# Sums in three steps, scores in two: replanning the interleave of an attention and a feed-forward network

## The chip, the cores and the metric

The kernel runs on one core of a Trainium2 chip. The metric is the device time of one execution in microseconds (us); a smaller number is better. The core has a matrix engine (TensorE, "PE" in the profile, with its weight loads as "PEld"), three engines for elementwise work (VectorE "DVE", ScalarE "ACT", GpSimd "POOL") and SyncE ("SP"), which issues DMAs. Each engine works through its own instructions in order and waits for others by semaphores.

## The reference, cut to what matters

For each of 8 batches and 8 heads (576 rows, head size 64, 32 memory slots):

```python
a = exp(phi - max(phi, axis=seq)); a = a / (sum(a, axis=seq) + 1e-9)  # softmax over the sequence
k_m = einsum('bhsm,bhsd->bhmd', a, k)          # sums over the sequence: 32 slots a head
v_m = einsum('bhsm,bhsd->bhmd', a, v)
scores = (q @ k_m.T) / sqrt(64)
attn = softmax(scores)                         # over the 32 slots
x = (attn @ v_m) as (4608, 512)
h = x @ w_in ; g = max(0.01 * h, h) ; out = g @ w_out     # 512 -> 2048 -> 512
```

w_in and w_out come as 8-byte floats, which the kernel puts together from pairs of words; the other inputs have 4 bytes.

## The kernel before, in words

**Attention of a batch** is cut into steps `aB.X` (B is 0 to 7; "the third batch" is a2). phi, k, v and q are loaded (phi, kv0 to kv3, q0, q1). A1 to B3 make the exponentials of phi: VectorE takes maxima (A1), PE transposes and spreads them (A2, B0), ScalarE applies exp (B20). C10 are the sums k_m and v_m: 72 f32 products, each on a 64x32 tile of PE, eight tiles side by side, over nine slices j of the rows (`slots_of`, line 654; the trace counts 144 matmuls, two for each f32 product). C2 to D6 scale and transpose the results; D2 (line 346) spreads a maximum over the partitions, from a diagonal that VectorE makes in C4. Q0 and Q1 are VectorE's transpositions of q for the two groups of heads (line 772). E1 makes the scores for both groups: 48 f32 products on 32x32 tiles, twelve side by side, 96 matmuls in the trace (`scores`, line 793); its three PSUM buffers are the whole pool `ps_a`. E20 to E22 transpose the scores out of PSUM, S01 to S08 are the softmax.

**The feed-forward network** does not multiply by v_m first: steps `Wbj.p` fold v_m of batch b into the quarter j of w_in (line 909, also on 64x32 tiles), h and l split the result in two f16 halves. Then each group of 256 rows, quarter by quarter (k counts group and quarter), goes through `pk.i` (PE, up: six or twelve matmuls, line 1104), `vk.i` (ScalarE, leaky ReLU), `sk` (VectorE, four sums), `ck`, `lk` (f16 halves by ScalarE and VectorE), and `dk.n` (PE, down: seven steps of six matmuls of 256 columns, line 1172). `xG` and `zG` combine, scale and store a group. The first three groups of rows use an older form, `P`, `V`, `C`, `L`, `O`, `Z` (lines 993 and 1061).

**The order** of all steps is written out by hand in two strings, OPENING (up to about 105 us) and LATER. The program runs them word by word under a manual schedule, so the order of the words is the order of the instructions on each engine. Between engines only semaphores hold. `FB = 2` is the number of first batches that keep f32 folds.

Of the kernel before, what the change touches and what calls it, by code (L numbers as in the profile page):

```python
# [68 lines left out]
a2.phi a2.kv2 W01.h1 W01.h0 i0.k1 a2.kv3 W01.l0 i0.k0 W01.l1 i0.k2 o0.s0 Z0.0 a2.kv0 a2.A1 Z0.1  # L69
W11.p o0.m0 Z0.2 P8.0 o0.s1 W11.h0 o0.n0 a2.A2 V8.0 P8.1 W11.l0 W11.h1 P9.0 W11.l1 V8.1 a2.kv1  # L70
C8 P9.1 V9.0 L8 V9.1 o0.s2 W02.h1 O8.0 C9 W02.h0 W02.l1 o0.m1 W02.l0 o0.m2 O8.1 L9 o0.n1 W12.p
o0.n2 o0.s3 P10.0 W12.h1 o1.s0 P10.1 W12.l1 V10.0 o3.s3 P11.0 V10.1 a2.A3 W12.h0 O9.0 V11.0
W12.l0 o1.k0 C10 o1.k1 i0.l2 a2.B0 L10 P11.1 o1.k2 o1.l1 O9.1 V11.1 W03.h1 o1.l2 W03.h0 W03.l1
P12.0 o0.m3 W03.l0 o1.l0 W13.p V12.0 C11 O10.0 W13.h0 W13.h1 W13.l0 o1.m0 W13.l1 P12.1 L11
O10.1 V12.1 o0.n3 o1.n0 o1.s1 P13.0 C12 o1.m1 o1.s2 P13.1 V13.0 o1.n1 P14.0 L12 V13.1 O11.0
o1.s3 V14.0 C13 o1.m2 a2.B10 o2.k0 P14.1 o2.k1 o2.l0 O11.1 V14.1 o2.l1 o2.k2 o1.m3 o1.n2 a2.B20
P15.0 o2.l2 L13 O12.0 o1.n3 V15.0 o2.s0 C14 a2.C10 o2.m0 o2.s1 o2.n0 o2.m1 L14 P15.1 a2.q0
o2.n1 O12.1 o2.s2 V15.1 a2.B3 o2.m2 a2.q1 P16.0 o2.s3 a2.C2 V16.0 O13.0 C15 o3.k0 o2.n2 a3.phi
o3.k1 L15 P16.1 o3.k2 o3.l0 O13.1 V16.1 o3.l2 o2.m3 o3.l1 o3.s0 P17.0 C16 O14.0 o3.s1 V17.0 L16
o3.s2 P17.1 a2.C30 o3.m1 O14.1 a2.Q0 V17.1 o3.m3 o3.m2 o3.n3 P18.0 a2.C3k o3.n2 a2.D10 V18.0  # L80
o3.n1 o3.m0 O15.0 C17 a2.D3 a2.Q1 P18.1 L17 O15.1 V18.1 a2.C31 i0.l1 C18 a2.E1 Z1.0 a2.C4 Z1.1
L18 Z1.2 P19.0 i0.l0 O16.0 a2.E21 V19.0 a2.E20 i1.k1 a3.kv2 a2.E22 o2.n3 i1.k0 a2.D2 a2.S01
a2.D11 i1.k2 P19.1 a3.kv1 a2.D4 O16.1 V19.1 a2.S02 a2.D5 a3.kv0 P20.0 C19 a2.D6 L19 O17.0 V20.0
a3.kv3 a2.S03 i1.l0 i1.l1 W20.p a2.S04 P20.1 W20.h0 O17.1 V20.1 W20.h1 W20.l0 C20 P21.0 a2.S05
O18.0 V21.0 L20 W20.l1 a2.S06 P21.1 O18.1 V21.1 i1.l2 a2.S07 o3.n0 C21 W21.p i2.k1 a3.A1 a2.S08
P22.0 i2.k0 O19.0 V22.0 L21 i2.k2 W21.h0 W21.h1 a3.A2 P22.1 i2.l0 i2.l1 O19.1 V22.1 i2.l2 C22
i3.k1 P23.0 W21.l0 i3.l1 O20.0 V23.0 i3.k0 W21.l1 L22 i3.k2 W22.p i3.l0 P23.1 W22.h0 i3.l2
O20.1 W22.l0 V23.1 a3.A3 W22.h1 C23 W23.p W22.l1 L23 p0.0 W23.h0 a3.B0 os2 v0.0 W23.l0 O21.0
W23.h1 a3.B10 W23.l1 p0.1 O21.1 v0.1 a3.B20 a3.B3 a3.C10 p0.2 a3.q0 a3.C2 v0.2 O22.0 a3.C30
a3.C3k a3.C31 a3.q1 a3.C4 a3.D11 a3.D10 a3.D2 a3.D3 p0.3 a3.D4 a4.phi O22.1 v0.3 a3.Q0 a3.D5  # L90
c0.0 p1.0 s0 p1.1 v1.0 O23.0 v1.1 l0.0 c0.1 a3.Q1 p1.2 O23.1 v1.2 l0.1 a3.D6 a4.A1 p1.3 a3.E1
v1.3 Z2.2 Z2.0 s1 Z2.1 p2.0 p2.1 a3.E22 v2.0 d0.0 a3.E21 v2.1 a3.E20 c1.0 d0.1 a4.kv0 os3 W30.p
c1.1 l1.0 p2.2 W30.h0 l1.1 d0.2 a4.kv1 v2.2 W30.h1 d0.3 a3.S01 d0.4 p2.3 a4.kv3 W30.l1 d0.5
a3.S02 v2.3 d0.6 c2.0 p3.0 s2 a4.kv2 p3.1 v3.0 d1.0 v3.1 l2.0 c2.1 d1.1 W30.l0 p3.2 l2.1 W31.p
v3.2 a3.S03 d1.2 d1.3 W31.h0 a3.S04 d1.4 W31.h1 p3.3 d1.5 v3.3 W31.l0 d1.6 c3.0 s3 p4.0 p4.1
v4.0 l3.0 a4.A2 v4.1 d2.0 c3.1 a3.S05 d2.1 p4.2 l3.1 d2.2 v4.2 d2.3 a3.S06 d2.4 p4.3 W31.l1
d2.5 a4.A3 v4.3 a3.S07 d2.6 s4 a4.B0 p5.0 a3.S08 p5.1 a4.B10 v5.0 d3.0 v5.1 d3.1 x3.p c4.0 p5.2
d3.2 v5.2 c4.1 d3.3 x3.0 d3.4 a4.B20 x3.1 p5.3 l4.0 d3.5 v5.3 x3.2 a4.C10 c5.0 l4.1 l5.0 s5
d3.6 a4.q0 p6.0 p6.1 x3.3 v6.0 d4.0 a4.B3 v6.1 c5.1 d4.1 a4.q1 p6.2 d4.2 l5.1 v6.2 z3.1 a4.C2
d4.3 a5.phi a4.C30 z3.0 d4.4 a4.Q0 p6.3 a4.C3k d4.5 v6.3 a4.D10 c6.0 s6 d4.6 a4.D3 p7.0 l6.0  # L100
p7.1 v7.0 a4.Q1 d5.0 v7.1 c6.1 d5.1 p7.2 a4.C31 l6.1 d5.2 v7.2 a4.E1 a4.C4 a5.A1 d5.3 a5.kv0
d5.4 p7.3 a4.E20 a4.E22 d5.5 v7.3 a5.kv2 a4.E21 a4.D2 c7.0 s7 a4.D11 d5.6 p8.0 a5.kv1 l7.0 p8.1
v8.0 a4.S01 d6.0 v8.1 c7.1 d6.1 a5.kv3 p8.2 l7.1 d6.2 v8.2 d6.3 a4.S02 d6.4 p8.3 a4.D4 d6.5
v8.3 a4.D5 os4 W32.p s8 d6.6 W32.h0 p9.0 W32.h1 W32.l0 p9.1 v9.0 W32.l1 d7.0 v9.1 a4.D6 d7.1
x4.p c8.0 p9.2 d7.2 v9.2 c8.1 d7.3 x4.0 d7.4 a4.S03 x4.1 p9.3 l8.0 d7.5 v9.3 x4.2 W33.p c9.0
l8.1 d7.6 W33.h1 p10.0 W33.h0 W33.l1 p10.1 W33.l0 v10.0 d8.0 x4.3 v10.1 d8.1 s9 z4.0 p10.2 d8.2
v10.2 l9.0 c9.1 d8.3 d8.4 z4.1 l9.1 p10.3 d8.5 v10.3 W40.p c10.0 s10 d8.6 W40.h1 p11.0 W40.h0
l10.0 p11.1 v11.0 a4.S04 d9.0 v11.1 c10.1 d9.1 p11.2 l10.1 d9.2 v11.2 d9.3 a4.S05 d9.4 p11.3
W40.l0 d9.5 W40.l1 v11.3 W41.p a4.S06 c11.0 a5.A2 W41.h0 d9.6 s11 a4.S07 p12.0 p12.1 v12.0
l11.0 a4.S08 d10.0 v12.1 c11.1 d10.1 W41.l0 p12.2 W41.h1 l11.1 d10.2 v12.2 d10.3 d10.4 p12.3  # L110
# [12 lines left out]
v19.0 a5.S02 d17.0 v19.1 c18.1 d17.1 W50.l0 p19.2 W50.h1 l18.1 d17.2 v19.2 a5.S03 d17.3 W50.l1
d17.4 a5.S04 p19.3 d17.5 v19.3 W51.p c19.0 s19 d17.6 W51.h0 p20.0 W51.h1 l19.0 p20.1 v20.0
d18.0 a5.S05 v20.1 c19.1 d18.1 p20.2 l19.1 d18.2 v20.2 d18.3 a5.S06 d18.4 p20.3 W51.l1 d18.5
W51.l0 v20.3 d18.6 c20.0 s20 p21.0 p21.1 v21.0 l20.0 d19.0 v21.1 d19.1 x7.p c20.1 p21.2 d19.2
v21.2 a5.S07 d19.3 x7.0 d19.4 x7.1 p21.3 a5.S08 x7.2 d19.5 l20.1 v21.3 d19.6 c21.0 p22.0 p22.1
v22.0 d20.0 v22.1 d20.1 x7.3 p22.2 s21 d20.2 v22.2 d20.3 l21.0 c21.1 d20.4 p22.3 l21.1 d20.5
v22.3 z7.1 d20.6 s22 c22.0 p23.0 p23.1 v23.0 d21.0 l22.0 v23.1 c22.1 d21.1 p23.2 l22.1 d21.2
v23.2 z7.0 d21.3 d21.4 p23.3 d21.5 v23.3 d21.6 c23.0 s23 p24.0 p24.1 v24.0 l23.0 d22.0 v24.1  # L130
c23.1 a6.A2 d22.1 a6.A3 p24.2 l23.1 a6.B0 v24.2 d22.2 a6.B10 d22.3 d22.4 a6.B20 p24.3 d22.5
v24.3 a6.B3 W52.p c24.0 d22.6 W52.h1 p25.0 W52.h0 W52.l1 p25.1 W52.l0 v25.0 d23.0 s24 v25.1
a6.C10 x8.p l24.0 c24.1 l24.1 d23.1 a6.q0 a6.C2 p25.2 a6.C30 d23.2 v25.2 a6.C3k d23.3 x8.0
a6.q1 d23.4 x8.1 a6.D10 x8.2 a6.C31 p25.3 a6.D3 a6.Q0 a7.phi d23.5 v25.3 W53.p c25.0 s25 d23.6
W53.h1 p26.0 W53.h0 p26.1 W53.l1 v26.0 d24.0 W53.l0 v26.1 c25.1 d24.1 x8.3 l25.0 p26.2 d24.2
l25.1 v26.2 z8.1 d24.3 z8.0 d24.4 a6.Q1 p26.3 d24.5 v26.3 a6.E1 c26.0 s26 l26.0 c26.1 d24.6
a7.kv3 a6.E22 p27.0 l26.1 p27.1 v27.0 d25.0 a7.kv1 v27.1 a6.E21 d25.1 a6.E20 a6.C4 p27.2 a6.D11
a6.S01 v27.2 a7.kv2 a6.D2 d25.2 d25.3 a6.D4 d25.4 a7.kv0 a6.S02 a6.D5 p27.3 d25.5 a6.D6 v27.3
d25.6 c27.0 s27 W60.p p28.0 l27.0 p28.1 v28.0 a7.A1 d26.0 v28.1 c27.1 d26.1 p28.2 W60.h1 l27.1
d26.2 v28.2 a6.S03 d26.3 W60.l1 d26.4 os6 W60.h0 p28.3 a6.S04 d26.5 v28.3 d26.6 c28.0 s28 p29.0  # L140
# [1217 lines left out]
```

## Time and profile before

| | |
|---|---|
| median of 3 runs | 663.27 us (662.59 to 666.29) |
| the profiled execution's own time | 662.05 us |
| its span, first to last instruction | 659.8 us |
| PE busy | 642.2 us (97%) |
| PE weight loads busy | 481.8 us (73%) |
| VectorE busy | 519.2 us (79%) |
| ScalarE busy | 396.3 us (60%) |
| GpSimd busy | 31.1 us (5%) |
| granted TensorE clock, mean | 0.997 |

The profile shows one execution. Busy times are shares of the span; a matmul's end is modelled, so neighbouring matmuls overlap in it, and the pace is read from starts: the time from one step's first start to the next step's first start.

### The profile page before, as it was taken

To read this page: it belongs to the slowest core of one execution; us is meant where nothing else is said; L and a number is where in the kernel's file an instruction comes from. 1 tells how busy PE (TensorE), PEld (TensorE's weight loads), DVE (VectorE), ACT (ScalarE), POOL (GpSimd) and SP (SyncE) were. 2 spreads that over 40 slices of the span, in tenths; PEclk is the share of its full clock that TensorE was granted. 3 is DMA by queue.
4 is the path that set the end of the run, shared out by engine and by line. 5 is a ranking of instruction groups with operands and counts; after the bars stand their busy time and mean duration, and the time that the engine had idled before them with its cause. 6 is when DMAs were issued, how large, how long until landed. Compare 5 with 4: busy or idle time off the path is not lost.

```text
span 659.8 us, 17603 instructions
## 1 busy us (share of the span) xinstructions
PE 642.2 (97%) x7592; PEld 481.8 (73%) x7592; DVE 519.2 (79%) x857; ACT 396.3 (60%) x677; POOL 31.1 (5%) x43
## 2 busy tenths in 40 slices
...
GB/s 292 400 314 309 232 86 121 1 51 60 192 1 82 65 157 69 178 42 33 51 93 139 40 1 33 109 177 3 34 74 33 2 33 6 30 18 16 33 2 48
DMA packets 32605, 60.38 MB, mean 92 GB/s; under 512 B 4368, under 2 KB 14608, under 8 KB 32528
## 3 DMA queue, kind: packets, MB, share of 16 engines
q1 hardware_dynamic: 32432, 59.13, 29.6%
q8 instruction: 59, 0.97, 0.6%
q10 hardware_dynamic: 96, 0.13, 0.1%
...
## 4 chain that ended last, share of the span: by engine, by line
PE 91%; DVE 5%; ACT 1%; issue 1%; DMA 1%; SPq 0%; POOL 0%; DVEq 0%; ACTq 0%; POOLq 0%
PE po L1172 31%; PE ph L1104 21%; PE po L1061 14%; PE ph L993 8%; PE ph L1172 5%; PE pa L909 4%; PE pa L654 2%; PE pa L793 2%; PE po L1206 1%; PE pa L1260 1%; DMA arena<-in_moe_w_out_dram 1%; PE pa L605 0%; DVE tm L827 0%; PE pa L346 0%; DVE t L807 0%
## 5 line engine op out<-in xcount | busy, mean ns | idle before, releaser
L1172 PEld LDWEIGHTS <-arena 128*128 128x128 f16 x2184 | 210.4, 98 | 30.4 <-issue 7.4
L1120 ACT ACTIVATE wi<-ph,g_sc 128x256 f32<-128x256 f32 (+1 forms) x224 | 98.8, 465 | 171.1 <-PE ph L1104 168.4
L1104 PE MATMUL ph<-a,w_mem 128*128 128x256 f16 (+3 forms) x1440 | 144.7, 246 | 0.0
L1104 PEld LDWEIGHTS <-w_mem 128*128 128x128 f16 x1440 | 114.4, 98 | 14.4 <-issue 3.5
L1172 PE MATMUL po<-wo,arena 128*128 128x256 f16 x936 | 122.0, 273 | 0.0
L1172 PE MATMUL po<-arena 128*128 128x256 f16 x936 | 115.5, 273 | 0.0
L1061 PE MATMUL po<-wo,arena 128*128 128x512 f16 (+1 forms) x384 | 110.9, 434 | 0.0
L1149 DVE TENSOR_TENSOR arena<-arena 128x1024 f16<-128x1024 f32 x52 | 64.1, 1233 | 25.1 <-ACT arena L1145 25.0
L1149 DVE TENSOR_TENSOR arena<-wi,arena 128x768 f16<-128x768 f32 (+1 forms) x60 | 54.3, 905 | 10.7 <-ACT arena L1145 10.7
L1141 DVE TENSOR_TENSOR arena<-wi 128x256 f32<-128x256 f32 x104 | 39.9, 425 | 24.7 <-ACT wi L1120 24.6
L1145 ACT CAST arena<-arena 128x1024 f16<-128x1024 f32 x52 | 54.4, 1046 | 2.3 <-DVE arena L1141 2.3
L993 PE MATMUL ph<-a,w_mem 128*128 128x192 f16 (+2 forms) x304 | 53.7, 323 | 1.6 <-DVE a L852 1.6
L1061 PEld LDWEIGHTS <-arena 128*128 128x128 f16 x288 | 27.8, 98 | 29.9 <-DVE wo L419 0.8
L1145 ACT CAST arena<-wi 128x768 f16<-128x768 f32 (+1 forms) x60 | 46.5, 776 | 1.7
L1141 DVE TENSOR_TENSOR arena<-wi,arena 128x256 f32<-128x256 f32 x104 | 45.8, 440 | 1.8
L876 POOL TENSOR_TENSOR a<-t,a 128x384 f16<-128x384 f32 x22 | 22.7, 1053 | 444.6 <-ACT a L871 440.4
L1172 PE MATMUL ph<-wo,arena 128*128 128x256 f16 x312 | 42.6, 273 | 0.0
L1000 ACT ACTIVATE arena<-ph,g_sc 128x384 f32<-128x384 f32 x32 | 18.6, 582 | 26.3 <-PE ph L993 21.6
L1061 PEld LDWEIGHTS po<-wo,arena 128*128 128x128 f32 x96 | 17.6, 190 | 21.0 <-issue 19.1
L909 PE MATMUL pa<-wi,vT 64*32 64x512 f16 (+1 forms) x704 | 28.9, 420 | 0.5 <-ACT vT L742 0.5
L932 ACT ACTIVATE w_mem<-pa 128x512 f16<-128x512 f32 x40 | 22.8, 596 | 8.0 <-PE pa L909 7.1
L993 PEld LDWEIGHTS <-w_mem 128*128 128x128 f16 x240 | 20.6, 98 | 9.4 <-issue 3.6
...
## 6 DMA issues: line engine op xcount, KB each, us to landing
...
```

The lines of the kernel that those rows point to most:

```text
L876: nc.gpsimd.tensor_tensor(lo[:, tb], t2[:, tb], hi[:, tb], ALU.subtract)
L909: nc.tensor.matmul(pf[g][cols, :], lhs, rhs, start=(n == 0), stop=(n == len(passes) - 1), tile_position=(g * D, hh * M),)
L932: nc.scalar.activation(halves(w16(b, j), g)[:, 0], src["w"][g] if b else w32[j][g], AF.Copy, scale=ws)
L993: nc.tensor.matmul(ph[:, t0:t0 + n * SB], lhs, rhs, start=(m == 0), stop=(m == len(seq) - 1))
L1000: nc.scalar.activation(dst, ph, AF.Prelu, scale=sc, alpha=SLOPE)
L1061: nc.tensor.matmul(po, lhs, rhs, start=(f == 0 and m == 0), stop=(f == NQ * NF - 1 and m == len(seq) - 1),)
L1104: nc.tensor.matmul(ph[:, t0:t0 + n], lhs, rhs, start=(m == 0), stop=(m == len(seq) - 1))
L1120: nc.scalar.activation(dst, ph, AF.Prelu, scale=g_sc2[:, j:j + 1], alpha=SLOPE)
L1141: nc.vector.tensor_tensor(gt[:, x], y, z, op)
L1145: nc.scalar.copy(dst[:, 0], src)
L1149: nc.vector.tensor_tensor(dst[:, 1], src, dst[:, 0], ALU.subtract)
L1172: nc.tensor.matmul(acc, g[:, x, s, u], rhs, start=(h == 0 and j == 0 and u == 0 and m == 0), stop=(j == NQ - 1 and u == 1 and m == 2), ski ...
```

## The change

The code changes in two places, both for batches 2 to 7 only. C10 becomes C10, C11 and C12, each with three of the nine slices j. E1 becomes E1 with the first group of heads and E1b with the second. The products themselves, their number and their order within the step stay; results are accumulated in the same PSUM buffers.

```diff
-        def slots_of(kinds):
+        def slots_of(kinds, js=range(KJ)):
...
-            for j in range(KJ):
+            for j in js:
...
-            steps[f"{name}C10"] = lambda: slots_of((0, 1))
+            parts = 3 if b >= FB else 1
+            for x in range(parts):
+                js = range(x * KJ // parts, (x + 1) * KJ // parts)
+                steps[f"{name}C1{x}"] = lambda js=js: slots_of((0, 1), js)
...
-        steps[f"{name}E1"] = lambda: scores((1,) if b == 0 else range(NG))
+        steps[f"{name}E1"] = lambda: scores((1,) if b == 0 else range(NG) if b < FB else (0,))
+        if b >= FB:
+            steps[f"{name}E1b"] = lambda: scores((1,))
```

LATER is a new order of the same words with the new ones between; OPENING stays. The stretch of the sixth batch, before and after:

```diff
-x5.p c12.1 p13.2 d11.2 v13.2 a5.B20 d11.3 x5.0 d11.4 x5.1 a5.C10 x5.2 l12.1 a5.B3 p13.3 a5.q0
-d11.5 v13.3 d11.6 c13.0 a5.C2 x5.3 p14.0 a5.q1 s13 p14.1 v14.0 d12.0 v14.1 d12.1 l13.0 c13.1
-p14.2 a6.phi d12.2 l13.1 v14.2 z5.0 d12.3 z5.1 a5.C30 d12.4 p14.3 a5.Q0 d12.5 v14.3 d12.6 c14.0
-s14 p15.0 p15.1 v15.0 d13.0 l14.0 v15.1 c14.1 d13.1 a5.C31 p15.2 l14.1 a5.D11 v15.2 d13.2
-a5.C3k a5.Q1 d13.3 a5.D10 d13.4 a5.C4 a5.D3 p15.3 a6.A1 a5.D2 v15.3 d13.5 c15.0 d13.6 p16.0 s15
...
-l16.0 v17.1 a5.E1 x6.p c16.1 l16.1 d15.1 a6.kv3 p17.2 a5.E22 a5.E21 d15.2 v17.2 d15.3 x6.0
+a5.B20 d12.6 s14 p15.0 a5.C10 v15.0 a5.B3 c14.0 p15.1 a5.C11 v15.1 c14.1 d13.0 l14.0 a5.C12
+l14.1 d13.1 a5.q0 a5.C2 d13.2 a5.C30 p15.2 d13.3 a5.C31 v15.2 a5.q1 a5.C4 a5.C3k d13.4 p15.3
+a5.D10 v15.3 a6.phi c15.0 s15 d13.5 a5.D3 d13.6 p16.0 l15.0 p16.1 v16.0 a5.Q0 d14.0 v16.1 c15.1
+d14.1 d14.2 l15.1 a5.E1 a5.Q1 p16.2 d14.3 v16.2 d14.4 a6.A1 a5.E1b p16.3 a6.kv3 a5.E20 d14.5
```

The last words of the order, from p54.0 on, follow each other on PE as before.

## Rows read from the trace of the kernel before

**Rows 1.** The chain of waits that ended last, share of the span by engine.
```profile
PE 91%; DVE 5%; ACT 1%; issue 1%; DMA 1%; SPq 0%; POOL 0%; DVEq 0%; ACTq 0%; POOLq 0%
```
**Rows 2.** Busy time by stretch: start:end, length, each engine's busy us (instructions), clock, DMA.
```profile
105.00:350.00 245.00, 241.58 (x2930) 174.13 (x2930) 221.22 (x349) 142.47 (x244) 9.67 (x12) 1.00 0.29 80
350.00:655.00 305.00, 304.56 (x3751) 261.68 (x3749) 222.20 (x369) 176.28 (x317) 8.96 (x11) 1.00 0.16 44
```
**Rows 3.** PE's waits from 105 us on: line, releaser, us in total, times, longest.
```profile
PE pa L654 <- issue: 2.5, 2, 1.5
PE ph L1104 <- ACT wi L1120: 0.4, 1, 0.4
PE pa L346 <- DVE mdiag L341: 0.4, 1, 0.4
```
**Rows 4.** PE in time order, ordinary steps: start, us to modelled end, operation, count.
```profile
273.47 1.48 PE L1172 MATMUL po<-arena 128*128 128x256 f16 x12
274.79 0.82 PE L1104 MATMUL ph<-a,w_mem 128*128 128x256 f16 x6
```
**Rows 5.** The same view around the seventh batch's sums, then its transpositions D10.
```profile
417.24 0.82 PE L1172 MATMUL ph<-wo,arena 128*128 128x256 f16 x6
417.99 2.25 PE L654 MATMUL pa<-arena 64*32 64x128 f32 x144
420.17 0.50 PE L1172 MATMUL po<-wo,arena 128*128 128x256 f16 x3
...
423.58 0.60 PE L719 MATMUL pa<-ident,x_k 128*96 128x128 f32 x4
424.01 0.58 PE L1104 MATMUL ph<-a,w_mem 128*128 128x192 f16 x5
```
**Rows 6.** The same view around a fold.
```profile
414.46 0.84 PE L909 MATMUL pa<-wi,vT 64*32 64x512 f16 x24
415.24 0.39 PE L1172 MATMUL po<-arena 128*128 128x256 f16 x2
```
**Rows 7.** The same view: scores, batch 0's first half; the sixth batch's whole.
```profile
15.02 1.15 PE L793 MATMUL pa<-wi,kT 32*32 32x192 f32 x48 [0.67 <-ACT kT L736]
...
354.05 1.93 PE L793 MATMUL pa<-arena,kT 32*32 32x192 f32 x96
355.91 0.28 PE L1172 MATMUL po<-wo,arena 128*128 128x256 f16 x1
```
**Rows 8.** The same view, fourth and fifth batch's sums; idle time in brackets.
```profile
205.64 2.16 PE L654 MATMUL pa<-arena 64*32 64x128 f32 x133
209.34 0.44 PE L654 MATMUL pa<-arena 64*32 64x128 f32 x11 [1.55 <-issue]
209.71 0.83 PE L1104 MATMUL ph<-a,w_mem 128*128 128x256 f16 x6
...
255.68 2.20 PE L654 MATMUL pa<-arena 64*32 64x128 f32 x139
258.82 0.41 PE L654 MATMUL pa<-arena 64*32 64x128 f32 x5 [0.94 <-issue]
259.17 0.50 PE L1172 MATMUL po<-wo,arena 128*128 128x256 f16 x3
```
**Rows 9.** Engine totals; instruction packets (span, 206 to 209.5); a stretch as rows 2.
```profile
PE 642.2 (97%) x7592; PEld 481.8 (73%) x7592; DVE 519.2 (79%) x857; ACT 396.3 (60%) x677; POOL 31.1 (5%) x43
...
q8 instruction: 59, 0.97, 0.6%
...
q8 instruction: 1, 0.02, 2.1%
...
209.34:258.81 49.48, 48.21 (x637) 37.09 (x637) 44.12 (x73) 28.00 (x50) 3.21 (x4) 1.00 0.34 100
```
**Rows 10.** VectorE in time order around the sixth batch's second transposition of q.
```profile
339.61 1.77 DVE L772 STREAM_TRANSPOSE arena<-arena 96x1536 f32<-96x1536 f32 x1
...
341.84 0.29 DVE L341 TENSOR_SCALAR mdiag<-ident,m 128x128 f32<-128x128 f32 x1
```

More of the change, by code (lines that the diff above doesn't have):

```diff
@@ L68 @@
 LATER = """
[L69 to L110, printed above, removed]
@@ L123 @@
[L123 to L140, printed above, removed]
@@ L183 @@
-d54.0 c55.1 l55.1 d54.1 d54.2 d54.3 d55.0 d55.1 d55.2 d55.3 end
+a2.phi a2.kv2 W01.h1 W01.h0 i0.k0 a2.kv1 i0.k1 W01.l1 W01.l0 i0.k2 o0.s0 Z0.0 a2.kv0 a2.A1
+o0.m0 Z0.1 W11.p Z0.2 P8.0 o0.s1 W11.h0 o0.n0 P8.1 V8.0 W11.l0 P9.0 o0.s2 a2.kv3 V8.1 W11.h1 C8
+P9.1 V9.0 L8 o0.m1 a2.A2 V9.1 W11.l1 O8.0 W02.h0 C9 W02.h1 W02.l0 o0.m2 W02.l1 O8.1 L9 o0.n1
+W12.p o0.n2 o0.s3 P10.0 W12.h0 o1.s0 a2.A3 P10.1 V10.0 W12.l0 P11.0 V10.1 o3.s3 W12.h1 O9.0 C10
+V11.0 W12.l1 o1.k1 L10 o1.k0 P11.1 o1.l1 o1.k2 O9.1 o0.m3 o1.l0 V11.1 o1.l2 W03.h0 C11 W03.h1
@@ new lines @@
+a2.B0 W03.l0 P12.0 o1.m0 W03.l1 O10.0 V12.0 L11 o0.n3 o1.n0 W13.p o1.s1 P12.1 a2.B10 W13.h0
+O10.1 V12.1 W13.l0 W13.h1 o1.m1 W13.l1 P13.0 a2.B20 o1.n1 o1.s2 P13.1 V13.0 C12 a2.C10 o1.s3
+V13.1 o1.m2 L12 P14.0 o2.k0 C13 a2.C11 V14.0 o1.n2 O11.0 o2.k1 o2.l0 o2.k2 o2.l1 o1.m3 a2.C12
+o2.l2 P14.1 L13 a2.q0 o1.n3 O11.1 V14.1 o2.s0 C14 o2.m0 a2.q1 o2.s1 P15.0 o2.n0 O12.0 L14 V15.0
+o2.m1 o2.s2 o2.n1 o2.m2 P15.1 a2.B3 O12.1 V15.1 o2.s3 a3.phi a2.C2 C15 o3.k1 P16.0 o2.n2 o3.k2
+O13.0 o3.l1 V16.0 o3.k0 o3.l2 L15 o2.m3 P16.1 o3.l0 O13.1 V16.1 o3.s0 C16 o3.s1 P17.0 L16 O14.0
@@ new lines @@
+V17.0 o3.s2 a2.C30 o3.m2 o3.m3 a2.Q0 P17.1 o3.m1 O14.1 a2.C3k o3.n3 V17.1 o3.n2 o3.m0 o3.n1
+a2.D10 C17 P18.0 a2.D3 a2.Q1 O15.0 V18.0 L17 a2.C31 P18.1 i0.l1 a2.E1 V18.1 a2.C4 O15.1 C18
+i0.l2 L18 a2.E1b Z1.2 i0.l0 Z1.1 P19.0 a2.E20 Z1.0 a2.E21 a2.D2 V19.0 a2.E22 O16.0 a2.D4 i1.k0
+i1.k1 a2.S01 a3.kv0 a2.D11 i1.k2 P19.1 i1.l1 a2.D5 O16.1 a3.kv2 V19.1 a2.S02 C19 a2.S03 P20.0
+a3.kv3 a2.D6 L19 W20.p V20.0 a2.S04 O17.0 W20.h1 a3.kv1 W20.h0 W20.l1 P20.1 a2.S05 O17.1 V20.1
+W20.l0 a2.S06 P21.0 C20 i1.l2 O18.0 V21.0 L20 a2.S07 i1.l0 P21.1 a2.S08 o3.n0 i2.k1 W21.p V21.1
@@ new lines @@
+O18.1 i2.k0 i2.k2 W21.h0 P22.0 C21 W21.h1 i2.l0 O19.0 V22.0 L21 i2.l2 P22.1 i2.l1 O19.1 W21.l0
+V22.1 i3.k1 W21.l1 C22 i3.k0 W22.p i3.l1 i3.k2 P23.0 i3.l0 W22.h0 O20.0 i3.l2 V23.0 L22 W22.h1
+W22.l1 P23.1 W22.l0 o2.n3 O20.1 V23.1 a3.A1 W23.p C23 p0.0 W23.h0 os2 a3.A2 L23 v0.0 O21.0
+W23.h1 W23.l0 W23.l1 a3.A3 p0.1 O21.1 v0.1 a3.B0 p0.2 a3.B10 O22.0 v0.2 a3.B20 p0.3 a3.B3
+a3.C10 v0.3 O22.1 c0.0 s0 a3.C11 l0.0 c0.1 p1.0 a3.C12 v1.0 l0.1 p1.1 a3.q0 a3.C2 v1.1 O23.0
+a3.C30 a3.C3k a3.C31 a3.q1 a3.C4 a3.D11 a3.D10 a3.D2 a3.D3 p1.2 a3.D4 a4.phi O23.1 v1.2 a3.Q0
@@ new lines @@
+a3.D5 p1.3 a3.D6 a3.Q1 p2.0 v1.3 a3.E1 v2.0 Z2.2 s1 p2.1 Z2.0 a3.E1b Z2.1 v2.1 a4.A1 d0.0 c1.0
+d0.1 c1.1 d0.2 a4.kv3 l1.0 p2.2 d0.3 l1.1 v2.2 d0.4 a4.kv0 a3.E21 p2.3 a3.E22 d0.5 a3.E20 v2.3
+os3 d0.6 c2.0 a4.kv2 s2 W30.p p3.0 W30.h0 l2.0 p3.1 a4.kv1 v3.0 a3.S01 d1.0 v3.1 c2.1 d1.1
+W30.l0 d1.2 W30.h1 l2.1 p3.2 W31.p v3.2 a3.S02 d1.3 W31.h1 d1.4 W31.h0 W30.l1 a3.S03 p3.3
+W31.l1 d1.5 W31.l0 v3.3 d1.6 c3.0 s3 p4.0 p4.1 v4.0 l3.0 d2.0 v4.1 c3.1 d2.1 a3.S04 d2.2 p4.2
+d2.3 l3.1 v4.2 d2.4 a3.S05 p4.3 d2.5 v4.3 d2.6 a3.S06 c4.0 p5.0 s4 p5.1 v5.0 d3.0 v5.1 a3.S07
```

131 lines of the change are left out of this document (83 added, 48 removed).

## The prediction, made before the result was known

> **What bounds the kernel now.** I first read the busy time by stretch. The written-out later order, which is all that the change touches, fills 105 to 655 us. In it PE is busy for 241.58 of the first 245 us and for 304.56 of the other 305 [rows 2]; the differences are 3.42 and 0.44, so PE is idle for 3.86 us in 550. The chain of waits says the same: 91% of the span is PE's own work [rows 1]. VectorE is the next, at 221.22 of 245 us in the first stretch and 222.20 of 305 in the second [rows 2]. Then I read PE's waits in the later order: 2.5 us of the 3.86 are called "issue" and stand at line 654, the sums, twice; 0.4 waits for ScalarE near the end, 0.4 for VectorE ahead of D2 [rows 3], the rest is shorter. So only two things can move the time: what PE's own steps cost, and the waits, above all the two at line 654.
>
> **Does "busy" mean full pace?** A row of matmuls that starts at 273.47 holds 12 products of 256 columns and the next step starts at 274.79: 1.32/12 = 0.11 us each [rows 4]. That pace holds across ordinary steps, so PE's time is the sum of its steps, and a step that grows by x delays the end by x.
>
> **What a tiled step costs at its ends.** The sums work on eight 64x32 tiles at once, the scores on twelve of 32x32; all neighbours use the whole array. Ahead of the seventh batch's sums, six products start at 417.24 and should have been fed by 417.24 + 6 x 0.11 = 417.90, yet the sums start at 417.99: 0.1 us is lost on entering. The sums last from 417.99 to 420.17, 2.18 us [rows 5]. Their content: 144 matmuls in eight tiles are 18 in depth, of 128 columns f32. Four whole-array f32 matmuls of 128 columns take from 423.58 to 424.01, 0.108 each [rows 5], so 18 take 1.95. The remaining 0.23 is the end: the tiles run out one after another before the whole array may start.
>
> **Part 1, sums in three.** No matmul is added. Each third has 48 matmuls, 6 in depth: 6 x 0.108 + 0.23 = 0.88, three make 2.64 against 2.18: +0.46 a batch. Lower bound of the end: the folds (24 matmuls, 3 in depth, of 512 columns or 3 x 0.22 = 0.66) last from 414.46 to 415.24 = 0.78 [rows 6], an end of 0.12; with that a third would last 0.77 and three 2.31, +0.13. Nothing hides these, for PE has no slack. I take 0.44, nearer to the step itself. Six batches: +2.6 (0.8 to 2.8).
>
> **Part 2, scores in two.** The score step lasts 354.05 to 355.91 = 1.86 us [rows 7]. Half of its content is at least 0.93. Batch 0 already has its scores in halves: 48 matmuls from 15.02, for 1.15 us to the modelled end of the last [rows 7]; the whole step's row says 1.93 where 1.86 passed to the next start, so 1.08 at most. Two halves cost 0 to 0.30 more; I take 0.2, nearer to the half that exists. Six batches: +1.2 (0 to 1.8).
>
> **Part 3, the entries.** In the new order every part has a whole-array step on either side (a5: C10 p15.1 C11 d13.0 C12; E1 p16.2 d14.3 d14.4 E1b), so 2 + 1 = 3 entries are added in each of six batches: 18 x 0.1 = +1.8. Lower end 0, if the new neighbours were hidden in the fill; upper 2.0.
>
> **Part 4, the two "issue" waits.** The sums of the fourth batch run from 205.64 to 209.71 = 4.07, those of the fifth from 255.68 to 259.17 = 3.49, against 2.18: 1.89 + 1.31 = 3.2 us lost. In each, PE stops with nothing to wait for, 133 and 139 matmuls in, and goes on at 209.34 and 258.82 [rows 8]. What is special there is the rate. Every matmul has its weight load, so the sums use 288 instructions in 2.18 us, where ordinary steps use 2 in 0.11, 40 in the same time. Instructions come by a queue of their own: 59 packets of 0.97 MB in all, 16 KB each, for 2 x 7592 instructions of PE [rows 9], or 257 a packet. From the end of the first stop to the end of the second there are 637 matmuls and 637 weight loads [rows 9]; with a few semaphore instructions that is 5 x 256. So both stops lie on the edge of a packet, and a packet is under way in the first (206 to 209.5 us [rows 9]). I read them as PE using up a packet inside the sums faster than the next comes. The instructions came 3.7 us after the first sums' start, and 3.1 after the second's. In the new order the same 256 instructions are 96 + some 14 + 96 + some 14 + the rest of the last third: 0.98 + 0.65 + 0.98 + 0.65 + 0.3 = 3.6 us at the fastest, and longer where the step between is one of 1.9 us. So both stops should go and none come: -3.2 (bounds 0 and -3.2).
> The Trainium skill ("Runtime: NRT & Kernel Launch", Instruction fetch mechanics) also has blocks of 16 KiB and 256 instructions, but calls the cost of crossing one mostly hidden; by that the 3.2 us would belong to something else and could stay. The trace shows 2.5 us of idle PE exactly there, so for the sum I follow the rows; the page's reading speaks for the third rival below.
>
> **Part 5, the replanned order.** The work on the other engines is the same, every step once. Without the two stops, 3.86 - 2.5 = 1.4 us of waits remain in the later order. The one ahead of D2 of the sixth batch goes: VectorE had put its 1.77 us transposition of q (339.61) before the diagonal that D2 needs (341.84) [rows 10]; in the new order that transposition, Q1, comes behind E1, which needs only Q0. The wait of 0.4 at the end stays, for the last steps are unchanged. New is that Q0 and Q1 stand three or four PE steps (2 us) ahead of E1 and E1b, where they stood half a group of rows ahead. PSUM is as full as before, but the scores hold all three shared buffers for some 2 us longer. Bounds -1.4 and +2; I take -0.4. DMA issues are the same ones in other places, and the queue of SP is mostly free in this stretch; I count nothing for them.
>
> **Sum:** 2.6 + 1.2 + 1.8 - 3.2 - 0.4 = +2.0 us on the profiled execution's 662.05: 664.05. That execution is the lowest of the four known (662.59, 663.27 and 666.29 are the others; the two in the middle average 662.9), and what is forecast is a median, so I add 0.5, about half of what lies between: **664.5 us**, 0.2% above the median of before. Less than 0.5%, 3.3 us, can't be told from no change here: same is 660.0 to 666.6. The likeliest case's own range is 662.5 to 666.5.
>
> **Rivals.**
> 1. *The ends cost little, the waits all go.* If thirds and halves cost nothing beyond their content (both lower bounds near 0) and only the entries are paid: 1.8 - 3.2 - 1.4 = -2.8, 659.8 with the 0.5; less if entries hide too. For it: no row shows so short a group of f32 tiles among whole-array steps, and the folds' end is half as long as the sums'. Against: the folds have an end all the same, and no slack covers it. 7%.
> 2. *Slower: q's transpositions become late.* Place: E1 and E1b, in each of six batches, behind Q0 and Q1 (1.77 us on VectorE [rows 10]) with some 2 us of PE work between. If what stands before them on VectorE is late by its usual wait for ScalarE, each half waits up to 1.77 and on average perhaps half: 6 x 0.9 = 5.3 more, 669.8. It decides from 0.4 us a batch on, where 664.5 becomes 666.9. For: VectorE is 90% busy in the first stretch [rows 2]. Against: after 350 us it is 73% busy, and three of the six batches lie there. 10%.
> 3. *The stops stay or move.* If they come from something other than the dense run of instructions, the change does not reach them: 664.5 + 3.2 = 667.7. For: four other sums of the same shape have none, so density alone doesn't make one. Against: the 5 x 256 between the two. 7%.
> The forecast has the remaining 76%.
>
> **Chances.** Faster by over 0.5% takes rival 1 at its better end and little else: 7%. Slower takes rivals 2 and 3, 17%, and nearly nothing of the forecast: 17%. Same: 76%. The range of 8 in 10 takes in rival 3 and the bounds -2.8 to +5 of the parts but not rival 2's full price: 661.0 to 667.7.
>
> **What would show it.** In the changed trace: PE pieces of 48 matmuls at line 654 with about 0.88 us to the next step's start, and 0.1 us before each; halves of about 1.03 us at the scores' line; no "issue" wait at line 654, and PE idle for under 2 us between 105 and 655 us, while the span is some 2 us longer, all of it as PE busy time. The forecast is wrong if thirds take under 0.78, if PE waits for VectorE or ScalarE at E1 or E1b, or if an "issue" wait of over 0.5 us remains.

## The result, and the profile after

The changed kernel takes 667.1 us (median of 16 runs, 665.56 to 669.28); the kernel before, in as many runs on the same chip, 663.61 us. The ratio is 1.005 with a 95% interval of 1.0039 to 1.0061: half a per cent slower, 2.6 to 4.0 us. The profiled execution's span went from 659.8 to 664.7 us.

That span difference of 4.9 us is not all the change's. I split it where the later order begins: at the first matmul of its first fold, 105.15 us before and 107.14 us after. The opening's words are the same in both kernels, and over eight kernels that share its instructions the later order began anywhere from 105.15 to 108.55 us. So the 2.0 us at the opening are within what the same opening varies by, one execution of each kernel. The later order, from that matmul to the last one's start, took 549.95 us before and **552.82 us** after: **+2.87 us**. This length is what I compare from here on; it is free of the opening's spread, and TensorE's granted clock in it is 1.00 in both.

Chain of waits after, by engine [as rows 1]:

```profile
PE 89%; DVE 4%; DMA 2%; ACT 2%; issue 1%; SPq 0%; POOL 0%; DVEq 0%; ACTq 0%; POOLq 0%
```

Busy time by stretch after, columns as in [rows 2]:

```profile
105.00:350.00 245.00, 243.95 (x2944) 171.58 (x2943) 217.53 (x343) 143.05 (x245) 10.10 (x12) 1.00 0.29 80
350.00:659.90 309.90, 308.98 (x3742) 263.25 (x3741) 227.49 (x378) 177.21 (x319) 8.78 (x11) 1.00 0.16 43
```

PE is idle for 1.05 + 0.92 us where it was idle for 3.86, and yet the end is later: PE waits less, but its steps have grown by more. Its waits after, from 105 us on [as rows 3]:

```profile
PE ph L1110 <- ACT wi L1126: 0.9, 2, 0.5
PE po L1178 <- DVE obs L1193: 0.4, 1, 0.4
PE pa L731 <- DVE x_v L704: 0.3, 1, 0.3
PE pa L797 <- DVE arena L776: 0.3, 1, 0.3
```

The two "issue" stops at the sums are gone. What took their place stands in the time order of PE. The fifth batch's sums [as rows 5, 8], in three parts with an ordinary step between (start, us to the modelled end, count):

```profile
266.30 0.94 PE L655 MATMUL pa<-arena 64*32 64x128 f32 x48
267.17 0.83 PE L1110 MATMUL ph<-a,w_mem 128*128 128x256 f16 x6
267.93 0.94 PE L655 MATMUL pa<-arena 64*32 64x128 f32 x48
268.80 0.83 PE L1178 MATMUL ph<-wo,arena 128*128 128x256 f16 x6
269.56 0.94 PE L655 MATMUL pa<-arena 64*32 64x128 f32 x48
270.43 0.39 PE L1178 MATMUL po<-wo,arena 128*128 128x256 f16 x2
```

Each third lasts 0.87 us from its start to the next step's (266.30 to 267.17), 2.61 together against 2.18 whole. The six matmuls between last 0.76 (267.17 to 267.93) where six at the free pace last 0.65: the entry of 0.1. The same batch's scores in halves [as rows 7]:

```profile
276.65 0.41 PE L1110 MATMUL ph<-a,obs 128*128 128x192 f16 x3
277.34 1.14 PE L797 MATMUL pa<-arena,kT 32*32 32x192 f32 x48 [0.28 <-DVE arena L776]
278.41 0.35 PE L1110 MATMUL ph<-a,w_mem 128*128 128x64 f16 x6
...
281.82 1.15 PE L797 MATMUL pa<-arena,kT 32*32 32x192 f32 x48
282.90 0.50 PE L1178 MATMUL po<-arena 128*128 128x256 f16 x3
```

A half lasts 1.07 to 1.08 us, so two are 2.16 against 1.86. The 0.28 in brackets is the one place where PE waits for a transposition of q.

### The profile page after: what moved, and what is told of

Read it like the earlier page. It is cut to its first block, busy times and chain, and to the rows that moved or that the text cites. A ratio compares the mean times of both kernels' runs of the same rounds, so it can differ in the third digit from the quotient of the medians.

```text
span 664.7 us, 17625 instructions
## 1 busy us (share of the span) xinstructions
PE 648.0 (97%) x7592; PEld 480.6 (72%) x7592; DVE 518.7 (78%) x857; ACT 395.8 (60%) x677; POOL 31.3 (5%) x43
## 4 chain that ended last, share of the span: by engine, by line
PE 89%; DVE 4%; DMA 2%; ACT 2%; issue 1%; SPq 0%; POOL 0%; DVEq 0%; ACTq 0%; POOLq 0%
PE po L1178 31%; PE ph L1110 21%; PE po L1067 12%; PE ph L999 7%; PE ph L1178 5%; PE pa L915 3%; PE pa L655 3%; PE pa L797 2%; DMA arena<-in_moe_w_out_dram 2%; PE po L1212 1%; PE pa L1266 1%; DMA arena<-in_q_dram 1%; ACT arena L396 1%; PE pa L606 0%; ACT arena L385 0%
## 5 line engine op out<-in xcount | busy, mean ns | idle before, releaser
L1178 PEld LDWEIGHTS <-arena 128*128 128x128 f16 x2184 | 209.5, 98 | 32.4 <-issue 9.5
L1178 PE MATMUL po<-arena 128*128 128x256 f16 x936 | 122.3, 273 | 0.0
L1155 DVE TENSOR_TENSOR arena<-wi,arena 128x768 f16<-128x768 f32 (+1 forms) x60 | 52.9, 881 | 10.4 <-ACT arena L1151 10.4
L776 DVE STREAM_TRANSPOSE arena<-arena 96x1536 f32<-96x1536 f32 x14 | 24.6, 1765 | 3.3 <-DMA arena<-in_q_dram 1.8
```

Of the source, the lines that this page charges most:

```text
L776: nc.vector.transpose(flat, ld["q", g].rearrange("p hh j d -> p (hh j d)"))
L1155: nc.vector.tensor_tensor(dst[:, 1], src, dst[:, 0], ALU.subtract)
L1178: nc.tensor.matmul(acc, g[:, x, s, u], rhs, start=(h == 0 and j == 0 and u == 0 and m == 0), stop=(j == NQ - 1 and u == 1 and m == 2), ski ...
```

## The experiments

All lengths are of the later order, start of its first matmul to start of its last, in one profiled execution; medians and ratios are of all executions, the ratios against the kernel before on the same chip. An "edge" is the place in PE's stream of instructions where one packet of 256 ends and the next begins.

| kernel | begins at | length | median | ratio, 95% interval |
|---|---|---|---|---|
| before | 105.15 | 549.95 | 663.61 | 1 |
| changed | 107.14 | 552.82 | 667.1 | 1.005 (1.0039 to 1.0061) |
| e1 parts adjacent | 106.85 | 550.00 | 663.89 | 0.9992 (0.9978 to 1.0007) |
| e2 sums whole | 107.70 | 550.61 | 664.66 | 1.0008 (0.9995 to 1.002) |
| e3 scores whole | 106.33 | 552.30 | 666.6 | 1.0044 (1.003 to 1.0057) |
| e4 both whole | 108.55 | 549.85 | 664.22 | 1.0007 (0.9995 to 1.0018) |
| e5 edges moved by 96 | 113.21 | 547.49 | 667.78 | 1.0056 (1.0034 to 1.0078) |
| e6 edges moved by 140 | 118.84 | 550.18 | 674.69 | 1.0158 (1.0134 to 1.0183) |
| e7 sums whole, early | 106.85 | 550.48 | 664.13 | 1.0005 (0.9992 to 1.0018) |
| e8 cuts in the old order | 106.22 | 555.50 | 669.66 | 1.0095 (1.0072 to 1.0119) |
| e9 edges moved by 208 | 112.10 | 547.34 | 665.11 | 1.0016 (1.0 to 1.0031) |
| e10 edges moved late, by 96 | 108.65 | 547.69 | 661.15 | 0.9948 (0.993 to 0.9967) |
| e11 changed, edges at sums | 106.42 | 553.56 | 667.12 | 1.0047 (1.003 to 1.0064) |

**e1: is it the cut or what stands between?** The changed code with the old order, parts adjacent.

```diff
-x5.p c12.1 p13.2 d11.2 v13.2 a5.B20 d11.3 x5.0 d11.4 x5.1 a5.C10 x5.2 l12.1 a5.B3 p13.3 a5.q0
+x5.p c12.1 p13.2 d11.2 v13.2 a5.B20 d11.3 x5.0 d11.4 x5.1 a5.C10 a5.C11 a5.C12 x5.2 l12.1 ...
```

> The old order, with the three parts of the sums and the two of the scores directly behind one another. Measure: the later order's length, from the first matmul of its first fold to the last matmul of the kernel (before: 105.15 to 655.10 = 549.95 us; changed: 107.14 to 659.96 = 552.82). Theory (a part costs only where whole-array work stands on both sides): as before, 549.5 to 550.5, ratio to before 0.999 to 1.001, and the two issue stops stand in the same two batches' sums (fourth and fifth), since the instructions and their places are the same. Rival 1 (cutting a step costs by itself, more semaphores and instructions): 553 or more, at least 3 us longer. Rival 2 (the stops are chance and not tied to the place of an instruction in the stream): none, or in other batches.

Measured: 550.00 us, ratio 0.9992. A cut between parts that stay neighbours is free. And both stops are back, after the same number of matmuls as in [rows 8]:

```profile
207.53 2.16 PE L651 MATMUL pa<-arena 64*32 64x128 f32 x133
211.06 0.44 PE L651 MATMUL pa<-arena 64*32 64x128 f32 x11 [1.37 <-issue]
...
257.40 2.20 PE L651 MATMUL pa<-arena 64*32 64x128 f32 x139
260.54 0.41 PE L651 MATMUL pa<-arena 64*32 64x128 f32 x5 [0.94 <-issue]
```

They are no chance: 133 and 139 matmuls in, in another execution of another build.

**e2 to e4: undo the cuts one at a time in the new order.** All parts stand where the last one stood.

```diff
-a5.B20 d12.6 s14 p15.0 a5.C10 v15.0 a5.B3 c14.0 p15.1 a5.C11 v15.1 c14.1 d13.0 l14.0 a5.C12
+a5.B20 d12.6 s14 p15.0 v15.0 a5.B3 c14.0 p15.1 v15.1 c14.1 d13.0 l14.0 a5.C10 a5.C11 a5.C12
...
-d14.1 d14.2 l15.1 a5.E1 a5.Q1 p16.2 d14.3 v16.2 d14.4 a6.A1 a5.E1b
+d14.1 d14.2 l15.1 a5.Q1 p16.2 d14.3 v16.2 d14.4 a6.A1 a5.E1 a5.E1b
```

> The new order, but all three parts of the sums stand together where the last stood; the scores stay in halves. Theory: the drains at the ends of thirds (18 x 0.87 against 6 x 2.18 = 2.6) and 12 entries (12 x 0.105 = 1.3) go: 552.8 - 3.9 = 548.9 us for the later order, ratio to before 0.998 to 1.000. The instruction packets' edges fall about 100 or more instructions behind the start of each batch's sums, so that less than a packet is used up inside; no issue stop. Rival (the stops come with whole sums, wherever the edges fall): two stops or so, 1.3 to 1.9 us each, 551.5 to 552.5.

> The new order, but both halves of the scores stand where the second stood; the sums stay in thirds. Theory: 12 halves of 1.08 against 6 x 1.86 (1.8) and 6 entries (0.6) go: 552.8 - 2.4 = 550.4 us. Rival (the halves hide a late transposition of q, the second group's, which now holds up the whole step): PE waits for VectorE ahead of the scores in the fourth, fifth and sixth batch, together up to 2.3 us, and 552.7 remains.

> The new order with sums and scores whole, each where its last part stood. Theory: the savings of the two one-sided kernels add up: 552.8 - 3.9 - 2.4 = 546.5 us, 3.4 below before, of which 3.2 are the two stops that this order does not have; ratio to before 0.994. With the waits for q's second transposition up to 548.8, ratio 0.998. Rival (the new order's interleave needs the parts: longer tiled steps starve ScalarE and VectorE and PE waits for them elsewhere): 550 or more without any issue stop.

Measured: 550.61, 552.30 and 549.85. The savings came short by 1.7, 1.9 and 3.4 us, and not by stops (none is in the later order of these traces), and hardly by q (0.5 us in one place in e2, where the changed kernel has 0.3; nothing in e3 and e4). PE's busy time in the later order did fall, from 550.9 to 547.2, 549.1 and 545.4 us; its idle time rose from 2.0 to 3.4, 3.2 and 4.4, which is most of what is missing. e4 is nearest to its rival, which had named such waits. e2 around the sixth batch:

```profile
334.21 0.82 PE L1106 MATMUL ph<-a,w_mem 128*128 128x256 f16 x6
335.65 0.82 PE L1106 MATMUL ph<-a,w_mem 128*128 128x256 f16 x6 [0.62 <-ACT wi L1122]
```

This is p15.0 and then p15.1. In the new order v15.0 (ScalarE) comes between the two, and PE's second step does not start before v15.0 has ended (335.13 + 0.47 = 335.60). In the changed kernel C10 stands in that gap. e3 has the same with the scores, 2.4 us in four waits:

```profile
PE ph L1106 <- ACT wi L1122: 2.4, 4, 0.9
```

So the new order spends the parts as cover for waits which it makes itself; the old order has p15.0 p15.1 v15.0 and no such wait. My rival for e3 had the size (552.7) but named the wrong partner (q instead of v).

**e7: whole sums, at the first part's place.**

```diff
+a5.B20 d12.6 s14 p15.0 a5.C10 a5.C11 a5.C12 v15.0 a5.B3 c14.0 p15.1 v15.1 c14.1 d13.0 l14.0
```

> The changed kernel with all three parts of the sums where the first stood; the scores stay in halves. In the kernel with the sums at the last part's place PE waited 0.79 us twice between two up steps of one group, where a part of the sums had stood between them. Theory: those waits are gone, the packets' edges fall at instruction 126 or later of each sums, so no stop: 552.82 - 2.7 (ends) - 1.3 (12 entries) = 548.8 us, ratio to before 0.997 to 0.999. Rival (the waits in the new order come anyway, since the parts had covered others as well): 550.4 or more.

Measured: 550.48, so the rival held. The waits of e2 went, but p1.1 now waits for the leaky ReLU v1.0 and C2 for VectorE's B3, which later parts had covered, 0.6 us each:

```profile
PE ph L1106 <- ACT wi L1122: 1.5, 3, 0.6
PE pa L668 <- DVE r1k L629: 0.6, 1, 0.6
```

**e8: the cuts alone, in the old order.**

```diff
-a5.C10 x5.2 l12.1 a5.B3 p13.3 a5.q0 d11.5 v13.3
+a5.C10 x5.2 l12.1 a5.B3 p13.3 a5.C11 d11.5 a5.C12 a5.q0 v13.3
...
-a5.E1 x6.p c16.1 l16.1 d15.1 a6.kv3 p17.2
+a5.E1 x6.p c16.1 l16.1 d15.1 a5.E1b a6.kv3 p17.2
```

> The old order with only the cuts: C11 after the next PE step behind C10, C12 after one more, E1b after the next PE step behind E1 (q0 and C2, which must follow the sums, move behind C12 where they stood before it). Theory: both stops go (-3.2), ends of thirds +2.6, ends of halves +1.8, 18 entries +1.9, other waits as before: 549.95 + 3.1 = 553.0 us (552.3 to 553.8), ratio 1.003 to 1.006: the whole loss comes from the cuts, and the replanning is worth 0 to 0.5. Rival (the cuts in the old order bring new waits that the replanning was needed for): 555 or more.

Measured: 555.50, ratio 1.0095, the rival's value. PE's busy time is 551.5 us, 0.6 above the changed kernel's; its idle time is 4.0 us against 2.0. That is mostly two new waits, 2.1 us where the old order has D11 (line 727) close behind the sums and 0.9 ahead of the seventh batch's D2:

```profile
213.17 0.33 PE L668 MATMUL pa<-ident,r1k 128*128 128x128 f32 x1
215.64 0.33 PE L727 MATMUL pa<-ident,x_v 128*128 128x128 f32 x1 [2.13 <-DVE x_v L700]
```

The later part of the sums had pushed C2 behind the work that covered VectorE's scaling. So the cuts need the replanning, and it is worth 555.5 - 552.8 = 2.7 us to them.

e8 shows one thing more. By the count of PE's records its fourth and fifth batch's sums begin at the same instruction as in the kernel before, to one; there the whole sums stopped [rows 8]. The thirds do not:

```profile
207.74 0.95 PE L651 MATMUL pa<-arena 64*32 64x128 f32 x48
208.63 0.83 PE L1106 MATMUL ph<-a,w_mem 128*128 128x256 f16 x6
209.39 0.94 PE L651 MATMUL pa<-arena 64*32 64x128 f32 x48
```

**e5, e6: what are the stops?** The kernel before, with small products in place of one idle product at the very start, so that every later instruction of PE stands 96 (25 products, e5) or 140 places (36, e6) further on. The later order's words are untouched.

```diff
+    def packet_shift(n):
...
+        for x in range(n):
+            g, hh = 0, x % HP
+            rows, cols = slice(g * D, (g + 1) * D), slice(hh * M, (hh + 1) * M)
+            nc.tensor.matmul(
+                pi[cols, g, 0:D], ones[rows, cols], ones[rows, 0:D], start=True, stop=True,
+                tile_position=(g * D, hh * M),
+            )
...
-        steps[f"z.{n}"] = lambda n=n: idle_products(n)
+        steps[f"z.{n}"] = lambda n=n: idle_products(n) if n < 4 else packet_shift(25)
```

> The kernel before with one of the first four idle products in the opening replaced by 25 small ones, 96 instructions of PE more ahead of everything else; the later order is untouched. The edges of PE's instruction packets, every 256 instructions, move by 96: in the sums of the six later batches from instruction 17, 11, 23, 142, 163 and 63 to 177, 171, 183, 46, 67 and 223. Theory (a stop comes only where an edge lies within the first 30 or so of the 288 instructions, so that the next edge falls inside too): no issue stop in any batch, later order 549.95 - 3.2 = 546.7 us (546.2 to 547.4), ratio to before 0.994 to 0.997. Rival (the stops belong to these two batches, through the loads of q or phi around them): both stay, 549.95.

> The same with 36 small products, 140 instructions more. The edges fall at instruction 133, 127, 139, 2, 23 and 179 of the six batches' sums. Theory: the stops of the fourth and fifth batch vanish and come back in the sixth and seventh (near 322 and 417 us), 1 to 2 us each; later order 549 to 550.5 us, ratio to before 0.998 to 1.001. Rival (the batch decides, not the edge): the fourth and fifth keep theirs, the sixth and seventh stay at 2.18 us.

Measured: 547.49, 0.1 above the theory's range, and 550.18, within it; the ratios, 1.0056 and 1.0158, missed theirs. In e5 the fourth batch's sums run through in one row of 144, 2.20 us:

```profile
213.69 2.26 PE L654 MATMUL pa<-arena 64*32 64x128 f32 x144
215.89 0.28 PE L1104 MATMUL ph<-a,w_mem 128*128 128x256 f16 x1
```

In e6 the stops stand in the sixth and the seventh batch, where no kernel had them before:

```profile
334.36 2.03 PE L654 MATMUL pa<-arena 64*32 64x128 f32 x128
338.11 0.45 PE L654 MATMUL pa<-arena 64*32 64x128 f32 x16 [1.72 <-issue]
...
430.62 2.20 PE L654 MATMUL pa<-arena 64*32 64x128 f32 x139
433.74 0.41 PE L654 MATMUL pa<-arena 64*32 64x128 f32 x5 [0.92 <-issue]
```

The place in the stream decides, not the batch. The whole kernels became slower all the same, in part because the opening has sums too, and the moved edges fell into those. Two stops in e5 up to 120 us, the second in batch 0's scores:

```profile
PE pa L654 <- issue: 2.2, 1, 2.2
PE pa L793 <- issue: 1.4, 1, 1.4
```

and three of together 9.7 us in e6 (7.5 in batch 0's two sums, 2.2 in the second batch's). I had not worked out the opening's edges before these two runs. In the second batch's sums the stop came after 132 matmuls in e5 and after 110 in e6: 22 matmuls or 44 instructions earlier, as the shift has it.

```profile
78.12 0.84 PE L654 MATMUL pa<-arena 64*32 64x128 f32 x34 [2.24 <-issue]
```

The rule that I tested, an edge within the first 30 instructions, is too simple, though. In this case the edge lies at instruction 220. And the third batch's sums, with an edge at 17 by the count in e5's expectation, lost nothing before (2.18 us) and 0.2 us in e1 (2.38).

The packets themselves settle it. They are in the traces as transfers of 16 KB on queue q8; with the edges counted back from the stops, this is when the packet that an edge needs was under way and when PE passed that edge (us):

| sums | transfer | PE passes the edge | after the landing |
|---|---|---|---|
| before, third batch, no stop | 140.96 to 142.07 | 143.44 | 1.38 |
| before, fourth batch, stop | 206.71 to 207.91 | 209.34 | 1.43 |
| before, fifth batch, stop | 256.44 to 257.37 | 258.82 | 1.45 |
| e6, second batch, stop | 75.70 to 76.85 | 78.12 | 1.27 |
| e8, fourth batch, thirds | 208.92 to 209.88 | 212.56 | 2.68 |
| e8, fifth batch, thirds | 259.52 to 260.64 | 262.57 | 1.94 |

Of 759 such edges in the thirteen traces none is passed earlier than 1.23 us after the landing, and at the stops of the kernel before, e1, e5, e6, e9, e10 and e11 at sums and scores PE goes on 1.27 to 1.58 us after it. So PE stops where it comes to an edge before the packet is ready; the dense sums are where it comes early. When a transfer begins is the other half: in the third batch it began before the sums did (141.61), in the fourth and fifth 0.8 to 1.1 us after. Why is open.

**e9, e10: a version without stops.** e9 moves the edges by 208 from the start (54 small products for two of the idle ones). e10 moves only what follows 84 us, by 24 small products in the step that waits for the bounds' diagonal:

```diff
-            var["pm"] = ps_a.tile([P, NQ], F32, name="pa")
+            pm = ps_a.tile([P, D], F32, name="pa")
+            if kind == "i":
+                for x in range(24):
+                    cols = slice(x % HP * M, (x % HP + 1) * M)
+                    nc.tensor.matmul(
+                        pm[cols, :], ones[0:D, cols], ones[0:D, 0:D], start=True, stop=True,
+                        tile_position=(0, x % HP * M),
+                    )
+            var["pm"] = pm[:, 0:NQ]
```

> The kernel before with two of the first four idle products replaced by 54 small ones, 208 instructions of PE more at the very start. The edges of the packets then fall at instruction 207, 211 and 152 of the opening's three sums and at 65, 59, 71, 190, 211 and 111 of the later six; in no case within the first 30. Theory: no stop at line 654 in the opening (the shift by 96 had one of 2.2 us, that by 140 two of 7.5) nor later; later order 546.7 to 547.6 us, the whole 2 to 3 us below before, ratio 0.995 to 0.998. Rival (any shift is paid in the opening, by what PE does there in place of idle products): later order 547 but the ratio at 1.000 or above.

> The kernel before with 24 small products, 96 instructions, in the opening's wait for the diagonal of the bounds (1.0 us at 82 us), so that only the edges of what follows move: 177, 171, 183, 46, 67 and 223 in the later sums, as in the kernel with 96 at the start, while the opening's sums keep theirs. Theory: no stop anywhere, later order 546.7 to 547.6 us, and the small products cost 0 to 1 us of the opening; ratio 0.995 to 0.998. Rival: as for the other kernel of this call.

Measured: e9 547.34 us, but 1.0016 as a whole, as the rival has it: a stop of 2.7 us stands in batch 0's sums, where I had counted an edge but no stop, and the later order begins 7 us later than before, of which the stop explains a part only.

```profile
PE po L654 <- issue: 2.7, 1, 2.7
```

The stop comes after 103 of the 144 matmuls, which is the edge at instruction 207 that the expectation names; the packet's transfer ran from 11.85 to 13.13 us, and PE went on at 14.55. For the rest of the 7 us the record shows a companion that I had overlooked, the clock. The stretch from 10 to 40 us, before and in e9 [as rows 2]:

```profile
10.00:40.00 30.00, 23.93 (x409) 12.73 (x400) 24.24 (x43) 21.86 (x35) 3.20 (x5) 0.94 1.03 384
10.00:40.00 30.00, 22.92 (x431) 12.99 (x432) 21.07 (x40) 17.34 (x28) 2.25 (x3) 0.72 0.96 340
```

The mean granted clock there fell from 0.94 to 0.72 (a mixture of 2.4 GHz and 1.2 GHz), and it is 0.83 in e5 and 0.70 in e6. Of e9's twelve executions the one with a mean clock of 0.998 took 662.11 us, the eleven with 0.987 to 0.992 took 664.26 to 666.4. So part of what e5, e6 and e9 lost in the opening goes with a lower clock. That it is lower because idle products were taken from the start is not tested.

e10: 547.69 us and a median of 661.15 against 663.57 on its chip, ratio 0.9948 (0.993 to 0.9967). It beats both kernels. One stop of 1.0 us is left in its opening, at batch 0's scores; it stands ahead of the added products, and the kernels with the same instructions up to there lose up to 0.7 us at the same edge. From 105 us on, the sums' line (662 in this kernel) is absent from PE's waits; the longest are the old ones, and a short "issue" at another line:

```profile
PE ph L1112 <- ACT wi L1128: 0.4, 1, 0.4
PE pa L346 <- DVE mdiag L341: 0.4, 1, 0.4
PE po L1180 <- issue: 0.4, 1, 0.4
```

**e11: does the cut protect, or did the edges merely move?** In e2, e4 and e7 whole sums had no stop either: the new order puts the edges elsewhere, 98 instructions or more behind the start of each batch's sums by the count of PE's records. e11 is the changed kernel with e10's device and 52 products (208 instructions), which brings the edges to the start of four batches' sums.

> The changed kernel with 52 small products, 208 instructions, at the same place. The edges then fall at instruction 18, 16, 6 and 4 of the sums of the fourth, sixth, seventh and eighth batch, where the whole sums of the old order stopped for 1.3 to 1.9 us. Theory (the cut itself protects: with whole-array steps between, 256 instructions take 3.5 us and more): no stop, or none over 0.3 us; later order 552.5 to 553.5 us, as without the shift. Rival (the changed kernel has no stops only because its edges happen to fall elsewhere): stops of 1 us and more in these four batches' thirds, later order 555 us or more. The small products themselves may cost the opening up to 2 us, which this says nothing about.

Measured: 553.56 us, 0.7 above the changed kernel. One third is held up, by 0.5 us in its length (the packet landed at 440.38, PE went on at 441.78); the other three batches not at all:

```profile
437.91 0.94 PE L663 MATMUL pa<-arena 64*32 64x128 f32 x48
438.78 0.83 PE L1186 MATMUL po<-arena 128*128 128x256 f16 x6
439.54 0.94 PE L663 MATMUL pa<-arena 64*32 64x128 f32 x48
440.41 0.84 PE L1118 MATMUL ph<-a,w_mem 128*128 128x192 f16 x12
441.18 0.43 PE L663 MATMUL pa<-arena 64*32 64x128 f32 x10
441.78 0.85 PE L663 MATMUL pa<-arena 64*32 64x128 f32 x38 [0.17 <-issue]
```

So the cut does protect, though not wholly: 0.5 us in one of four batches here and nothing in e8, where whole sums with an early edge lost 1.3 to 2.0 in six cases of eight (the other two are the third batch's). It works by time, for PE needs longer to the edge: in e8 1.2 and 0.5 us were left over the 1.4 after the landing. In the changed kernel, as it is, the edges lie harmlessly anyway.

## Why the prediction came out as it did

It forecast 664.5 us and at most half a per cent either way; measured are 667.1 and +0.5%, in the range, but half a microsecond past the 666.6 where its "same" ended. By its own terms, in us of the later order:

| term | forecast | measured in the trace after |
|---|---|---|
| ends of thirds | +2.6 | 18 x 0.87 + 0.1 - 6 x 2.18 = +2.7 |
| ends of halves | +1.2 | 12 x 1.08 - 6 x 1.86 = +1.8 |
| entries | +1.8 | 18 more (30 against 12), 0.09 each = +1.7 |
| the two stops | -3.2 | -3.2 |
| all other waits | -0.4 | idle +0.6, steps that were not cut, entries aside, -0.7; together -0.1 |
| sum | +2.0 | +2.9 (whole length: +2.87) |

**Thirds and entries** were read right from [rows 5]. The 0.1 in the first line is one third with 0.99.

**The halves** are the term that was mis-sized. The upper bound, 1.08 from batch 0's half [rows 7], was the value itself, to 0.01; I took two thirds of the way to it with no row for doing so. The nearest row was at hand, and it was a measurement of the very same step.

**The stops** went as forecast, and what they are was read rightly: e1 repeats them, e5 and e6 move them by moving instructions, and the packets' landings fit. How they went was read in part only. The prediction gave the cut as what removes them and did not ask where the edges would lie in the new order; that order removes them by itself (e4), since it moves the edges. The cut would have done it too (e8; e11 but for 0.5 us), so the -3.2 had two causes, and the prediction named one. The Trainium skill ("Runtime: NRT & Kernel Launch", Instruction fetch mechanics) calls the cost of crossing an edge "mostly hidden". Most edges here do cost nothing; in these sums six stops of the later order cost 1.3 to 2.0 us each.

**The other waits** I took at -0.4 for the one ahead of D2 that goes. It went. New ones came: 0.28 for q ahead of the fifth batch's scores, 0.45 for a leaky ReLU of ScalarE and 0.41 for a sum of VectorE. PE's idle time without the stops went from 1.4 to 2.0 us, where 1.0 was forecast. That the line still comes to -0.1 was not foreseen: the steps that were not cut took 0.7 less, 0.55 of it at D2's own matmuls (1.99 us in all before, 1.44 after), whose weight loads had waited 1.5 us for VectorE's diagonal and now wait 0.3.

**A sign of its own.** The prediction called itself wrong if PE waits for VectorE at E1 or E1b. It does so once, the 0.28 us above: the second rival's mechanism, at about a twentieth of its price of 5.3 (six times half of 1.77). By that sign the step that took q's transpositions to be in time failed in one batch of six; its share of the miss is small beside the halves' 0.6.

**What I did not see** is that parts of a step can serve as cover. I priced each cut as pure loss apart from the stops. In e2 to e4 and e7 the savings came short by 1.7 to 3.4 us when parts were put together in the new order, mostly by waits that came back. That did not change the sum, since those waits are made by the same order, but it changed what undoing would bring.

**The rest** of the difference to 667.1 is the base: I started from 662.55 for the kernel before, and 16 runs have its median at 663.61. 663.61 + 2.9 = 666.5, and the ratio's interval, 2.6 to 4.0 us, holds 2.9. So of the 2.6 us between 664.5 and 667.1, 0.9 lies in the terms and 1.1 in the base; the last 0.6 is within the spread of the executions.

**The rivals.** The first (ends cost little) is refuted by the thirds' 0.87. The third (stops stay, for they come from something else) is refuted by e5, e6 and the trace after. The second came true in one place out of twelve.
